# Block-sparse attention followed by a Swish MLP on one core: dummy matmuls at the head, one AV bank for both heads, earlier casts, and output steps that lag into the next group

## The chip, the cores and the metric

The kernel runs on one core of a Trainium2 chip. The metric is the device time of one execution in microseconds (us). Each kernel is executed several times; every execution that is compared here is fast, unless it is said otherwise (slow is an execution over 1.5% above the fastest of the same kernel). "The profile" is one traced execution; the span that it reports is about 2 us shorter than the measured time.

Engines: PE does matmuls (and 128-column transposes by a matmul with an identity), ACT does activations, DVE is the vector engine, POOL the general engine, and SP only issues transfers (DMA).

## The reference

```python
# q, k, v: (4 batches, 8 heads, 768 rows, 64); float32
scores = q @ k.T / 8, masked by 32x32 blocks          # band, first/last, 3 sampled
attn   = softmax(scores);   x = (attn @ v)            # -> x: (3072 tokens, 512)
h = x @ w_in                                          # 512 -> 2048
out = (h * sigmoid(beta * h)) @ w_out                 # 2048 -> 512
```

## The kernel before

A "pair" is two heads of one batch; there are 16 pairs. The rows of the four batches are cut into eight tiles of 512 or 256 rows, and for each tile the four pairs of its batch are worked one after the other. While a tile's attention runs, the MLP ("MoE" in the code) of the 512 tokens that were finished before is woven in: 16 up-projection steps (`h_step`) and 16 output steps (`o_step`), four matmuls of 512 columns each.

```python
tiles = [(0, 0, 512), (0, 512, 256), (1, 0, 256), (1, 256, 512),
         (2, 0, 512), (2, 512, 256), (3, 0, 256), (3, 256, 512)]
sc_pool: 2 buffers of 2 PSUM banks;  av_pool: 1 bank;  mm_pool: 3 banks

def emit_cast(x):                       # float32 loads -> float16
    ... cast K, Q; for pairs x >= 5: two DMA transposes on the SP queue ...
    nc.vector.tensor_copy(out=va[:, :, :, 0:D], in_=vst...)       # V as well

def av_step(hh):                        # one head: AV, then its normalisation
    av = av_pool.tile([P, 4, D + 1], FP32, tag="av", name="av")
    for qc in range(nq):
        for kc in range(NC): nc.tensor.matmul(av[:, qc, :], ...)
    nc.vector.reciprocal(...); nc.vector.tensor_tensor(... op=ALU.mult)
return steps, [av_step(0), av_step(1), turn]       # turn: transpose x on PE

# for pair x of a tile: when is the next pair cast?  One pair ahead:
if b == 0 or (b == 1 and q0 == 0): nxt = x + 1 ...
elif q0 + n == S and b + 1 < B:    nxt = x + NPAIR
slots[0 ...].append(lambda: (emit_cast(nxt), load_upto(nxt + 3)))

# one group's MLP: all h_steps, then all o_steps, spread over the score steps
backlog = moe_steps(gi * 512, 512)
```

Each score step is two or three matmuls into one of two score buffers (`sc`), and one exponential on ACT (`et<-sc`).

The softmax here doesn't subtract the row's maximum and nothing guards it: scores larger than these inputs give would overflow.

Of the kernel before, what the change touches and what calls it, by code (L numbers as in the profile page):

```python
# [17 lines left out]
def kernel(  # L18
# [14 lines left out]
    BLK = 32  # L33
# [23 lines left out]
    AUG = P - D  # L57
# [62 lines left out]
    oh_tok = persist.tile([P, NC, AUG], FP16, name="oh_tok")  # L120
    mask16 = persist.tile([NB, AUG], FP16, name="mask16")

    def emit_first():
# [7 lines left out]
        for j in range(3):  # L131
            emit_load(0, j)


# [9 lines left out]
        nc.gpsimd.memset(mask16, 0.0)  # L144

        nc.gpsimd.memset(onehot, 1.0)
        nc.gpsimd.affine_select(out=onehot, in_=onehot, pattern=[[1, NC], [NC, P]],
                                compare_op=ALU.is_ge, fill=0.0, base=0,
                                channel_multiplier=-BLK)
        nc.gpsimd.affine_select(out=onehot, in_=onehot, pattern=[[-1, NC], [-NC, P]],  # L150
                                compare_op=ALU.is_ge, fill=0.0, base=BLK - 1,
                                channel_multiplier=BLK)

        nc.gpsimd.memset(oh_tok, 1.0)
        nc.gpsimd.affine_select(out=oh_tok, in_=oh_tok, pattern=[[1, NC], [-BLK, AUG]],
                                compare_op=ALU.is_ge, fill=0.0, base=0,
                                channel_multiplier=NC)
        nc.gpsimd.affine_select(out=oh_tok, in_=oh_tok, pattern=[[-1, NC], [BLK, AUG]],
# [5 lines left out]
        nc.gpsimd.tensor_copy(out=ident32, in_=identity[0:16, 0:16])  # L164

# [16 lines left out]
        nc.vector.tensor_scalar(out=mask16[:, 0:NB], in0=mask_blk, scalar1=1.0,  # L182
                                scalar2=-NEG, op0=ALU.subtract, op1=ALU.mult)
        for i in range(NSTG):
            for h in range(2):
                nc.scalar.copy(out=stg["k"][i][:, h, :, D:P], in_=oh_tok)
            if i == 0:
                ps = mm_pool.tile([P, NC, AUG], FP32, tag="mm", name="mkt")
                for c in range(NC):
                    nc.tensor.matmul(ps[:, c, :], lhsT=oh_flat[:, c * P:(c + 1) * P],  # L190
                                     rhs=mask16, start=True, stop=True)
            for h in range(2):
                nc.scalar.copy(out=stg["q"][i][:, h, :, D:P], in_=ps)
# [13 lines left out]
    def emit_cast(x):  # L207
        b, j = seq[x]
        kst, qst, vst = loaded.pop((b, j))
        kX, qX = sets[x % NSET]  # L210
        va = va_tiles[x % NVA]
        for name, st32, dst in (("k", kst, kX), ("q", qst, qX)):
            st16 = stg[name][x % NSTG]
            nc.vector.tensor_copy(out=st16[:, :, :, 0:D],
                                  in_=st32.rearrange("p h (c d) -> p h c d", d=D))
            if x >= N_PE_PREP:
                nc.sync.dma_start_transpose(
                    out=dst.rearrange("p h (c s) -> p (h c) s", s=P),
                    in_=st16.rearrange("p h c e -> p (h c e)"))
        nc.vector.tensor_copy(out=va[:, :, :, 0:D],  # L220
                              in_=vst.rearrange("p h (c d) -> p h c d", d=D))
        prepared[(b, j)] = (kX, qX, va)

    def emit_turn(x, name, h):
        kX, qX, _ = prepared[seq[x]]
        dst = kX if name == "k" else qX
        st16 = stg[name][x % NSTG]
        tp = mm_pool.tile([P, NC, P], FP16, tag="mm", name="tp")
        for c in range(NC):
            nc.tensor.transpose(out=tp[0:D + NB, c, :], in_=st16[:, h, c, 0:D + NB],  # L230
                                identity=identity)
        nc.vector.tensor_copy(out=dst[0:D + NB, h, :],  # L232
                              in_=tp[0:D + NB].rearrange("p c s -> p (c s)"))

    def attn_steps(b, j, q0, n):
# [5 lines left out]
        def step(hh, kc0):  # L241
            def run():
                kX, qX, _ = prepared[(b, j)]
# [18 lines left out]
        def av_step(hh):  # L262
            def run():
                _, _, va = prepared[(b, j)]
                if hh == 0:
                    xst["t"] = work_pool.tile([P, 4, P], FP16, tag="xst", name="xst")
                xstage = xst["t"]
                av = av_pool.tile([P, 4, D + 1], FP32, tag="av", name="av")
                for qc in range(nq):
                    for kc in range(NC):  # L270
                        et, i = ets[hh][kc]
                        nc.tensor.matmul(av[:, qc, :],  # L272
                                         lhsT=et[:, i * n + qc * P:i * n + (qc + 1) * P],
                                         rhs=va[:, hh, kc, 0:D + 1],
                                         start=(kc == 0), stop=(kc == NC - 1))
                recip = work_pool.tile([P, 4], FP32, tag="recip", name="recip")
                nc.vector.reciprocal(out=recip[:, 0:nq], in_=av[:, 0:nq, D])  # L277
                nc.vector.tensor_tensor(  # L278
                    out=xstage[:, 0:nq, hh * D:(hh + 1) * D],
                    in0=av[:, 0:nq, 0:D],  # L280
                    in1=recip[:, 0:nq].to_broadcast([P, nq, D]),
                    op=ALU.mult)
            return run

        def turn():
            xstage = xst["t"]
            xtp = mm_pool.tile([P, 4, P], FP16, tag="mm", name="xtp")
            for qc in range(nq):
                nc.tensor.transpose(out=xtp[:, qc, :], in_=xstage[:, qc, :],  # L289
                                    identity=identity)  # L290
            nc.vector.tensor_copy(  # L291
                out=xT_sb[:, j, b * S + q0:b * S + q0 + n],
                in_=xtp[:, 0:nq, :].rearrange("p c s -> p (c s)"))

        return steps, [av_step(0), av_step(1), turn]


    def moe_steps(t0, n):
# [21 lines left out]
        def o_step(ts, quarter):  # L320
            def run():
# [17 lines left out]
        return ([h_step(f) for f in range(N_FFC)]  # L339
                + [o_step(ts, qq) for ts in range(n // P) for qq in range(4)])  # L340
# [19 lines left out]


    a_list = []
    behind = []
    seen = {0}
    tok = 0
    for b, q0, n in tiles:
        for j in range(NPAIR):
# [4 lines left out]
            if b == 0 or (b == 1 and q0 == 0):  # L372
                if x + 1 < 2 * NPAIR and x + 1 not in seen and (
                        j < NPAIR - 1 or q0 + n == S):
                    nxt = x + 1
            elif q0 + n == S and b + 1 < B:
                nxt = x + NPAIR
            seen.add(nxt)
            slots = [[] for _ in steps]
            last = len(steps) - 1  # L380
            for i, f in enumerate(behind):
                slots[min(i + 1, last)].append(f)
            if nxt is not None:
                slots[0 if b == 0 or q0 == 0 else last].append(
                    lambda nxt=nxt: (emit_cast(nxt), load_upto(nxt + 3)))
# [14 lines left out]
        tok += n  # L400
    for f in behind:
        a_list.append((0.0, f))

    with tc.manual_schedule():
        emit_first()
        emit_cast(0)
        load_upto(3)
        for name in ("k", "q"):
            for h in range(2):
                emit_turn(0, name, h)  # L410
        emit_beta()
        marks = [i for i, (w, f) in enumerate(a_list) if f == "mark"]
        backlog, per, acc, gi = [], 0.0, 0.0, 0
        for i, (w, f) in enumerate(a_list):
            if f == "mark":
                while backlog:
                    backlog.pop(0)()
                backlog = moe_steps(gi * 512, 512)
# [4 lines left out]
                continue  # L423
            f()
            acc += per * w
            while acc >= 1.0 and backlog:
                backlog.pop(0)()
                acc -= 1.0
        while backlog:
            backlog.pop(0)()  # L430
        for m in moe_steps((n_group - 1) * 512, 512):
            m()
# [30 lines left out]
```

## Time and profile before

325.17 us (median of 3 runs, 325.03 to 325.48).

The page of the kernel before: busy time of each engine, and three rows of the timeline in 40 equal slices (tenths busy; PEclk is the granted clock).

```profile
PE 292.4 (91%) x2527; PEld 162.7 (50%) x2527; DVE 143.6 (44%) x336; ACT 221.4 (69%) x289; POOL 13.0 (4%) x32
...
PE   2898789868799999999999999989999999989995
...
ACT  4588879665374988675997567887667896456711
...
PEclk9999999997799999999999999999999999999999
```

PE is the busiest engine. Busy PE is not the same as PE at its rate, so I also counted work: in this trace a matmul at full clock starts 215 ns (512 columns), 108 ns (256), 56 ns (128) or 32 ns (65, the AV matmuls) after the one before it. A stage's *work* is the sum of these costs; its *stall* is its length minus its work. The stages below start with the first score matmul of a tile. Over the whole span this gives 276.6 us of work and 46.3 us of stall. (The prediction counted AV at 29 ns, which moves 3 us from work to stall; here it is 32 for all kernels.)

| stage (rows of the batch) | start | length | work | stall |
|---|---|---|---|---|
| head | 0 | 11.3 | 1.8 | 9.5 |
| T0: batch 0, 512 | 11.3 | 26.9 | 19.6 | 7.3 |
| T1: batch 0, 256 | 38.2 | 25.0 | 19.5 | 5.5 |
| T2: batch 1, 256 | 63.2 | 31.6 | 20.7 | 10.9 |
| T3 and T4: 512 each | 94.9 | 95.4 | 93.2 | 2.2 |
| T5 and T6: 256 each | 190.2 | 46.2 | 41.5 | 4.6 |
| T7: batch 3, 512 | 236.4 | 54.9 | 52.6 | 2.4 |
| tail (last MLP group) | 291.3 | 27.7 | 27.6 | 0.1 |
| end (last eviction, transfer) | 319.0 | 3.8 | 0 | 3.8 |

The list of waits of PE, before (total us, times, longest):

```profile
PE av L272 <- DVE xst L278: 8.4, 16, 1.1
...
PE sc L246 <- ACT et L252: 3.0, 8, 0.5
PE sc L246 <- DMA qX_98<-qstg_77: 2.5, 1, 2.5
PE sc L246 <- DMA qX_96<-qstg_78: 2.1, 1, 2.1
PE xtp L289 <- DVE xst L278: 1.7, 4, 0.7
```

AV of the second head waits for the normalisation of the first (`xst`), since there is one AV bank. Twice PE waits for a DMA transpose (`qX<-qstg`). In the timeline of PE (start, duration, what, and in brackets the idle time before it and what ended that) these look so:

```profile
68.53 0.55 PE L272 MATMUL av<-va_73,et 128*128 128x65 f16 x12 [1.14 <-DVE xst L278]
...
72.45 0.49 PE L246 MATMUL sc<-qX_96,kX_95 88*128 88x256 f16 x3 [2.06 <-DMA qX_96<-qstg_78]
...
82.33 0.49 PE L246 MATMUL sc<-qX_98,kX_97 88*128 88x256 f16 x3 [2.54 <-DMA qX_98<-qstg_77]
```

After each of the two transfers' waits the trace has 3.4 us at half clock (the two 7s in the PEclk row). The first exponential, in the timeline of ACT:

```profile
12.35 1.94 ACT L252 ACTIVATE et<-sc 128x1024 f16<-128x1024 f32 x2 [3.11 <-PE sc L246]
```

### The profile page before, as it was taken

What the parts mean: (1) busy time and instruction counts of PE and PEld (TensorE: products, weight loads), DVE (VectorE), ACT (ScalarE), POOL (GpSimd) and SP (SyncE); (2) the same over time, 40 slices, a digit from 0 to 9 for tenths busy, and PEclk for the clock granted to TensorE, in tenths of its full rate; (3) what the DMA queues carried; (4) which work ended last, traced back from release to release, by engine and by line L of the source; (5) the groups of instructions that cost most, each with busy time, mean ns of one, the idle gap of its engine ahead of it and who ended that gap; (6) DMA issues with size and microseconds to landing.
All of it is one profiled execution on the core that took longest, in us unless ns stands there. A gap on an engine that the chain in (4) does not pass through costs nothing.

```text
span 322.8 us, 6109 instructions
## 1 busy us (share of the span) xinstructions
PE 292.4 (91%) x2527; PEld 162.7 (50%) x2527; DVE 143.6 (44%) x336; ACT 221.4 (69%) x289; POOL 13.0 (4%) x32
## 2 busy tenths in 40 slices
PE   2898789868799999999999999989999999989995
PEld 2555455534455455545545556545654545554442
DVE  6676245765121657332654115785122653116800
ACT  4588879665374988675997567887667896456711
POOL 6080000000000000000000000000000000000000
PEclk9999999997799999999999999999999999999999
DMA  6969993467961478788000116964101000110011
GB/s 179 376 125 207 197 361 109 146 120 201 266 200 46 83 196 207 173 242 244 3 0 2 47 53 100 275 121 77 36 34 67 0 2 1 66 65 2 0 67 65
DMA packets 55376, 38.41 MB, mean 119 GB/s; under 512 B 35877, under 2 KB 52277, under 8 KB 55349
## 3 DMA queue, kind: packets, MB, share of 16 engines
q1 hardware_dynamic: 51092, 33.82, 38.0%
q0 software_dynamic: 4224, 4.19, 8.0%
q8 instruction: 20, 0.33, 0.4%
q14 instruction: 8, 0.06, 0.0%
q10 hardware_dynamic: 32, 0.01, 0.0%
HBM read 27.27 MB, written 6.29 MB: 104 GB/s over the span
## 4 chain that ended last, share of the span: by engine, by line
PE 72%; ACT 11%; DVE 9%; DMA 4%; issue 3%; SPq 1%; ACTq 0%
PE op L327 25%; PE hp L308 18%; PE sc L246 15%; PE av L272 11%; ACT et L252 7%; ACT t_sb L313 3%; DVE g L315 3%; DVE xst L278 2%; PE xtp L289 2%; DMA vst<-in_v_dram 2%; PE tp L230 1%; DMA qX_98<-qstg_77 1%; DMA qX_96<-qstg_78 1%; DVE recip L277 1%; ACT osb L332 1%
## 5 line engine op out<-in xcount | busy, mean ns | idle before, releaser
L252 ACT ACTIVATE et<-sc 128x1024 f16<-128x1024 f32 (+1 forms) x160 | 148.3, 942 | 67.5 <-PE sc L246 66.5
L308 PE MATMUL hp<-xT_sb,w_in_sb 128*128 128x512 f16 x384 | 94.9, 381 | 0.0
L327 PE MATMUL op<-w_out_sb,g 128*128 128x512 f16 x384 | 94.3, 383 | 0.0
L315 DVE SCALAR_TENSOR_TENSOR g<-t_sb,hp 128x512 f16<-128x512 f16 x96 | 65.1, 687 | 55.5 <-ACT t_sb L313 54.7
L313 ACT ACTIVATE t_sb<-hp,beta_h_sb 128x512 f16<-128x512 f32 x96 | 65.8, 698 | 9.0 <-PE hp L308 7.6
L327 PEld LDWEIGHTS <-g 128*128 128x128 f16 x384 | 37.4, 98 | 41.6 <-issue 0.9
L272 PEld LDWEIGHTS <-et 128*128 128x128 f16 x1152 | 43.6, 98 | 27.4 <-DVE xst L278 17.2
L308 PEld LDWEIGHTS <-w_in_sb 128*128 128x128 f16 x384 | 37.3, 97 | 39.4 <-issue 0.8
L277 DVE RECIPROCAL recip<-av 128x4 f32<-128x4 f32 (+1 forms) x64 | 11.1, 174 | 84.5 <-PE av L272 84.5
L246 PE MATMUL sc<-qX_96,kX_95 88*128 88x512 f16 (+1 forms) x96 | 23.9, 349 | 3.0 <-DMA qX_96<-qstg_78 2.1
L332 ACT ACTIVATE osb<-op 128x512 f32<-128x512 f32 x24 | 14.3, 596 | 17.3 <-PE op L327 17.1
L278 DVE TENSOR_TENSOR xst<-av,recip 128x256 f16<-128x256 f32 (+1 forms) x64 | 22.9, 358 | 2.2
L246 PE MATMUL sc<-qX_98,kX_97 88*128 88x512 f16 (+1 forms) x72 | 16.7, 331 | 3.2 <-DMA qX_98<-qstg_77 2.5
L291 DVE COPY xT_sb<-xtp 128x512 f16<-128x512 f16 (+1 forms) x32 | 11.4, 356 | 15.0 <-PE xtp L289 15.0
L246 PE MATMUL sc<-qX_100,kX_99 88*128 88x512 f16 (+1 forms) x72 | 16.6, 325 | 0.7 <-ACT et L252 0.7
L246 PE MATMUL sc<-qX_102,kX_101 88*128 88x512 f16 (+1 forms) x72 | 16.3, 325 | 0.8 <-ACT et L252 0.7
L246 PE MATMUL sc<-qX_104,kX_103 88*128 88x256 f16 (+1 forms) x72 | 16.5, 326 | 0.2 <-DVE qX_104 L232 0.2
L272 PE MATMUL av<-va_70,et 128*128 128x65 f16 x288 | 11.8, 194 | 2.6 <-DVE xst L278 2.6
L289 PEld LDWEIGHTS <-xst 128*128 128x128 f16 x96 | 7.3, 98 | 10.9 <-DVE xst L278 5.7
L246 PEld LDWEIGHTS <-kX_95 88*128 88x128 f16 x96 | 8.5, 103 | 7.9 <-issue 4.7
L289 PE MATMUL xtp<-identity,xst 128*128 128x128 f16 x96 | 10.7, 220 | 1.7 <-DVE xst L278 1.7
L272 PE MATMUL av<-va_74,et 128*128 128x65 f16 x216 | 9.1, 196 | 1.9 <-DVE xst L278 1.9
(77 smaller groups left out, 134.6 us busy)
## 6 DMA issues: line engine op xcount, KB each, us to landing
kst<-in_k_dram SPq DMA_DIRECT2D x16, 384.0 KB, 3.9
qst<-in_q_dram SPq DMA_DIRECT2D x16, 384.0 KB, 4.8
vst<-in_v_dram SPq DMA_DIRECT2D x16, 384.0 KB, 5.5
out_dram<-osb SPq DMA_DIRECT2D x24, 256.0 KB, 2.0
w_in_sb<-in_moe_w_in_dram POOLq DMA_DIRECT2D x4, 512.0 KB, 8.4
w_out_sb<-in_moe_w_out_dram POOLq DMA_DIRECT2D x4, 512.0 KB, 16.6
kX_95<-kstg_76 SPq DMA_TRANSPOSE x2, 3.8
qX_96<-qstg_78 SPq DMA_TRANSPOSE x2, 4.0
```

The source lines that it names most:

```text
L246: nc.tensor.matmul(sc[:, i * n:(i + 1) * n], lhsT=kX[0:D + NB, hh, (kc0 + i) * P:(kc0 + i + 1) * P], rhs=qX[0:D + NB, hh, q0:q0 + n], star ...
L252: nc.scalar.activation(out=et[:, 0:kn * n], in_=sc[:, 0:kn * n], func=AF.Exp, bias=0.0, scale=SCALE)
L272: nc.tensor.matmul(av[:, qc, :], lhsT=et[:, i * n + qc * P:i * n + (qc + 1) * P], rhs=va[:, hh, kc, 0:D + 1], start=(kc == 0), stop=(kc == ...
L277: nc.vector.reciprocal(out=recip[:, 0:nq], in_=av[:, 0:nq, D])
L278: nc.vector.tensor_tensor(out=xstage[:, 0:nq, hh * D:(hh + 1) * D], in0=av[:, 0:nq, 0:D], in1=recip[:, 0:nq].to_broadcast([P, nq, D]), op= ...
L289: nc.tensor.transpose(out=xtp[:, qc, :], in_=xstage[:, qc, :], identity=identity)
L291: nc.vector.tensor_copy(out=xT_sb[:, j, b * S + q0:b * S + q0 + n], in_=xtp[:, 0:nq, :].rearrange("p c s -> p (c s)"))
L308: nc.tensor.matmul(hp[:, 0:n], lhsT=w_in_sb[:, c, f * P:(f + 1) * P], rhs=xT_sb[:, c, t0:t0 + n], start=(c == 0), stop=(c == NPAIR - 1))
L313: nc.scalar.activation(out=t_sb[:, 0:n], in_=hp[:, 0:n], func=AF.Tanh, bias=0.0, scale=beta_h_sb[:, f:f + 1])
L315: nc.vector.scalar_tensor_tensor(out=g[:, f, 0:n], in0=t_sb[:, 0:n], scalar=1.0, in1=hp[:, 0:n], op0=ALU.add, op1=ALU.mult)
L327: nc.tensor.matmul(op, lhsT=g[:, f, ts * P:(ts + 1) * P], rhs=w_out_sb[:, f, :], start=(f == 0), stop=(f == N_FFC - 1))
L332: nc.scalar.activation(out=osb, in_=op, func=AF.Copy, bias=0.0, scale=0.5)
```

## The change

Its intent: bring PE's clock up before the first real work; take work out of the head; end the AV waits by letting both heads of a tile share one AV bank and one normalisation; cast earlier, so that DMA transposes are ready; and mix PE-heavy output steps between the ACT-heavy up-projections. The core of the diff, with cuts:

```diff
+    def emit_warm(n): ... n matmuls of 512 columns on zeros, into a score buffer
 def emit_first():
-        nc.gpsimd: onehot by two affine_selects;  oh_tok 64 columns wide
+        oh_tok 24 columns wide; onehot = PE transpose of oh_tok, copied by ACT
+        emit_warm(6); ... transposes, copy ...; emit_warm(6)     # before the mask product
 def emit_cast(x):
-        V cast here
+    def emit_cast_v(x): ... V cast, now with the next load at the pair's last step
 def emit_turn(x, name, h, on_act=False):      # first Q copies run on ACT
@@ AV
-        def av_step(hh):          # one head, up to 4 row chunks
+        def av_step(half):        # two row chunks, both heads
-                av = av_pool.tile([P, 4, D + 1], FP32, tag="av", name="av")
+                av = av_pool.tile([P, 2, 2, D + 1], FP32, tag="av", name="av")
...
-        return steps, [av_step(0), av_step(1), turn]
+        return steps, [av_step(half) for half in range(nq // 2)] + [turn]
@@ MLP steps
+    N_LATE = 8
+    def mix(hs, late): ... two late o_steps first, the others spread between the h_steps
-                backlog = moe_steps(gi * 512, 512)
+                hs, os = moe_steps(gi * 512, 512)
+                backlog = mix(hs, late) + os[:N_LATE]
+                late = os[N_LATE:]                      # 8 of 16 go to the next group
@@ which pair is cast
-            if b == 0 or (b == 1 and q0 == 0): nxt = x + 1 ...
+            if b == 0 and q0 == 0:
+                if j < NPAIR - 1: nxt = x + 1
+            elif b == 0 and j >= 2 or b == 1 and q0 == 0 and j < 2: nxt = x + 2
...
-                slots[min(i + 1, last)].append(f)
+                slots[1 + 2 * i if len(behind) == 2 or last == 5 else i + 1].append(f)
...
-                    lambda nxt=nxt: (emit_cast(nxt), load_upto(nxt + 3)))
+                    lambda nxt=nxt: emit_cast(nxt))
+                slots[last].append(lambda nxt=nxt: (emit_cast_v(nxt), load_upto(nxt + 3)))
@@ end
+    n_hold = 5      # output steps kept for between the last AV steps ("two")
-        for m in moe_steps((n_group - 1) * 512, 512): m()
+        for m in mix(hs, late) + os: m()
```

More of the change, by code (lines that the diff above doesn't have):

```diff
@@ L56 @@
     NSTG = 2
-    AUG = P - D
     va_tiles = []
@@ L119, with emit_warm @@
     oh_flat = onehot.rearrange("j c p -> j (c p)")
-    oh_tok = persist.tile([P, NC, AUG], FP16, name="oh_tok")
-    mask16 = persist.tile([NB, AUG], FP16, name="mask16")
+    oh_tok = persist.tile([P, NC, NB], FP16, name="oh_tok")
+    mask16 = persist.tile([NB, NB], FP16, name="mask16")
+    warm = persist.tile([P, 512], FP16, name="warm")
+    sc_warm = []
+    def emit_warm(n):
+        if not sc_warm:
+            sc_warm.append(sc_pool.tile([P, 1024], FP32, tag="sc", name="warm_ps"))
+        for _ in range(n):
+            nc.tensor.matmul(sc_warm[0][:, 0:512], lhsT=warm[:, 0:P], rhs=warm,
+                             start=True, stop=True)
     def emit_first():
@@ L132, in emit_first @@
             emit_load(0, j)
+        nc.vector.memset(warm, 0.0)
         dif = persist.tile([NB, NB], FP32, name="dif")
@@ L143, in emit_first @@
                        allow_small_or_imprecise_dtypes=True)
-        nc.gpsimd.memset(mask16, 0.0)
-        nc.gpsimd.memset(onehot, 1.0)
-        nc.gpsimd.affine_select(out=onehot, in_=onehot, pattern=[[1, NC], [NC, P]],
-                                compare_op=ALU.is_ge, fill=0.0, base=0,
-                                channel_multiplier=-BLK)
-        nc.gpsimd.affine_select(out=onehot, in_=onehot, pattern=[[-1, NC], [-NC, P]],
-                                compare_op=ALU.is_ge, fill=0.0, base=BLK - 1,
-                                channel_multiplier=BLK)
         nc.gpsimd.memset(oh_tok, 1.0)
-        nc.gpsimd.affine_select(out=oh_tok, in_=oh_tok, pattern=[[1, NC], [-BLK, AUG]],
+        nc.gpsimd.affine_select(out=oh_tok, in_=oh_tok, pattern=[[1, NC], [-BLK, NB]],
                                 compare_op=ALU.is_ge, fill=0.0, base=0,
                                 channel_multiplier=NC)
-        nc.gpsimd.affine_select(out=oh_tok, in_=oh_tok, pattern=[[-1, NC], [BLK, AUG]],
+        nc.gpsimd.affine_select(out=oh_tok, in_=oh_tok, pattern=[[-1, NC], [BLK, NB]],
                                 compare_op=ALU.is_ge, fill=0.0, base=BLK - 1,
@@ L164, in emit_first @@
         nc.gpsimd.tensor_copy(out=ident32, in_=identity[0:16, 0:16])
+        for i in range(NSTG):
+            for nm in ("k", "q"):
+                nc.gpsimd.memset(stg[nm][i][:, :, :, D + NB:P], 0.0)
+        emit_warm(6)
+        ohp = mm_pool.tile([P, NC, P], FP16, tag="mm", name="ohp")
+        for c in range(NC):
+            nc.tensor.transpose(out=ohp[0:NB, c, :], in_=oh_tok[:, c, :], identity=identity)
+        nc.scalar.copy(out=oh_flat, in_=ohp[0:NB].rearrange("j c p -> j (c p)"))
+        emit_warm(6)
         mask_blk = persist.tile([NB, NB], FP32, name="mask_blk")
@@ L181, in emit_first, with emit_more_columns @@
                                            op0=ALU.is_equal, op1=ALU.max)
-        nc.vector.tensor_scalar(out=mask16[:, 0:NB], in0=mask_blk, scalar1=1.0,
+        nc.vector.tensor_scalar(out=mask16, in0=mask_blk, scalar1=1.0,
                                 scalar2=-NEG, op0=ALU.subtract, op1=ALU.mult)
-        for i in range(NSTG):
-            for h in range(2):
-                nc.scalar.copy(out=stg["k"][i][:, h, :, D:P], in_=oh_tok)
-            if i == 0:
-                ps = mm_pool.tile([P, NC, AUG], FP32, tag="mm", name="mkt")
-                for c in range(NC):
-                    nc.tensor.matmul(ps[:, c, :], lhsT=oh_flat[:, c * P:(c + 1) * P],
-                                     rhs=mask16, start=True, stop=True)
-            for h in range(2):
-                nc.scalar.copy(out=stg["q"][i][:, h, :, D:P], in_=ps)
+        for h in range(2):
+            nc.scalar.copy(out=stg["k"][0][:, h, :, D:D + NB], in_=oh_tok)
+        ps = mm_pool.tile([P, NC, NB], FP32, tag="mm", name="mkt")
+        for c in range(NC):
+            nc.tensor.matmul(ps[:, c, :], lhsT=oh_flat[:, c * P:(c + 1) * P],
+                             rhs=mask16, start=True, stop=True)
+        for h in range(2):
+            nc.scalar.copy(out=stg["q"][0][:, h, :, D:D + NB], in_=ps)
+    def emit_more_columns():
+        for i in range(1, NSTG):
+            for nm in ("k", "q"):
+                for h in range(2):
+                    nc.scalar.copy(out=stg[nm][i][:, h, :, D:D + NB],
+                                   in_=stg[nm][0][:, h, :, D:D + NB])
     def emit_beta():
@@ L219, in emit_cast, with emit_cast_v, emit_turn @@
                     in_=st16.rearrange("p h c e -> p (h c e)"))
+        prepared[(b, j)] = (kX, qX, va, vst)
+    def emit_cast_v(x):
+        _, _, va, vst = prepared[seq[x]]
         nc.vector.tensor_copy(out=va[:, :, :, 0:D],
                               in_=vst.rearrange("p h (c d) -> p h c d", d=D))
-        prepared[(b, j)] = (kX, qX, va)
-    def emit_turn(x, name, h):
-        kX, qX, _ = prepared[seq[x]]
+    def emit_turn(x, name, h, on_act=False):
+        kX, qX, _, _ = prepared[seq[x]]
         dst = kX if name == "k" else qX
@@ L231, in emit_turn @@
                                 identity=identity)
-        nc.vector.tensor_copy(out=dst[0:D + NB, h, :],
-                              in_=tp[0:D + NB].rearrange("p c s -> p (c s)"))
+        copy = nc.scalar.copy if on_act else nc.vector.tensor_copy
+        copy(out=dst[0:D + NB, h, :], in_=tp[0:D + NB].rearrange("p c s -> p (c s)"))
     def attn_steps(b, j, q0, n):
@@ L242, in run @@
             def run():
-                kX, qX, _ = prepared[(b, j)]
+                kX, qX, _, _ = prepared[(b, j)]
                 sc = sc_pool.tile([P, 1024], FP32, tag="sc", name="sc")
@@ L260, in attn_steps @@
         xst = {}
-        def av_step(hh):
+        def av_step(half):
             def run():
-                _, _, va = prepared[(b, j)]
-                if hh == 0:
-                    xst["t"] = work_pool.tile([P, 4, P], FP16, tag="xst", name="xst")
-                xstage = xst["t"]
-                av = av_pool.tile([P, 4, D + 1], FP32, tag="av", name="av")
-                for qc in range(nq):
-                    for kc in range(NC):
-                        et, i = ets[hh][kc]
-                        nc.tensor.matmul(av[:, qc, :],
-                                         lhsT=et[:, i * n + qc * P:i * n + (qc + 1) * P],
-                                         rhs=va[:, hh, kc, 0:D + 1],
-                                         start=(kc == 0), stop=(kc == NC - 1))
-                recip = work_pool.tile([P, 4], FP32, tag="recip", name="recip")
-                nc.vector.reciprocal(out=recip[:, 0:nq], in_=av[:, 0:nq, D])
+                _, _, va, _ = prepared[(b, j)]
+                if half == 0:
+                    xst["t"] = work_pool.tile([P, 4, 2, D], FP16, tag="xst", name="xst")
+                av = av_pool.tile([P, 2, 2, D + 1], FP32, tag="av", name="av")
+                for i in range(2):
+                    qc = half * 2 + i
+                    for hh in range(2):
+                        for kc in range(NC):
+                            et, m = ets[hh][kc]
+                            nc.tensor.matmul(av[:, i, hh, :],
+                                             lhsT=et[:, m * n + qc * P:m * n + (qc + 1) * P],
+                                             rhs=va[:, hh, kc, 0:D + 1],
+                                             start=(kc == 0), stop=(kc == NC - 1))
+                recip = work_pool.tile([P, 2, 2, 1], FP32, tag="recip", name="recip")
+                nc.vector.reciprocal(out=recip, in_=av[:, :, :, D:D + 1])
                 nc.vector.tensor_tensor(
-                    out=xstage[:, 0:nq, hh * D:(hh + 1) * D],
-                    in0=av[:, 0:nq, 0:D],
-                    in1=recip[:, 0:nq].to_broadcast([P, nq, D]),
+                    out=xst["t"][:, half * 2:half * 2 + 2],
+                    in0=av[:, :, :, 0:D],
+                    in1=recip.to_broadcast([P, 2, 2, D]),
                     op=ALU.mult)
@@ L288, in turn @@
             for qc in range(nq):
-                nc.tensor.transpose(out=xtp[:, qc, :], in_=xstage[:, qc, :],
+                nc.tensor.transpose(out=xtp[:, qc, :], in_=xstage[:, qc].rearrange("p h d -> p (h d)"),
                                     identity=identity)
@@ L337, in o_step @@
             return run
-        return ([h_step(f) for f in range(N_FFC)]
-                + [o_step(ts, qq) for ts in range(n // P) for qq in range(4)])
+        return ([h_step(f) for f in range(N_FFC)],
+                [o_step(ts, qq) for ts in range(n // P) for qq in range(4)])
     tiles = [(0, 0, 512), (0, 512, 256), (1, 0, 256), (1, 256, 512),
@@ L359, in load_upto, with mix @@
             n_loaded[0] += 1
+    N_LATE = 8
+    def mix(hs, late):
+        res, rest = late[:2], late[2:]
+        done = 0
+        for i, h in enumerate(hs):
+            res.append(h)
+            while done < len(rest) and done * len(hs) < (i + 1) * len(rest):
+                res.append(rest[done])
+                done += 1
+        return res
     a_list = []
     behind = []
-    seen = {0}
     tok = 0
@@ L371 @@
             nxt = None
-            if b == 0 or (b == 1 and q0 == 0):
-                if x + 1 < 2 * NPAIR and x + 1 not in seen and (
-                        j < NPAIR - 1 or q0 + n == S):
+            if b == 0 and q0 == 0:
+                if j < NPAIR - 1:
                     nxt = x + 1
-            elif q0 + n == S and b + 1 < B:
+            elif b == 0 and j >= 2 or b == 1 and q0 == 0 and j < 2:
+                nxt = x + 2
+            elif b > 0 and q0 + n == S and b + 1 < B:
                 nxt = x + NPAIR
-            seen.add(nxt)
             slots = [[] for _ in steps]
@@ L400 @@
         tok += n
+    n_hold = 5
     for f in behind:
         a_list.append((0.0, f))
+        a_list.append((0.0, "two"))
     with tc.manual_schedule():
@@ L406 @@
         emit_cast(0)
-        load_upto(3)
         for name in ("k", "q"):
             for h in range(2):
-                emit_turn(0, name, h)
+                emit_turn(0, name, h, on_act=(name == "q"))
+        emit_more_columns()
+        emit_cast_v(0)
+        load_upto(3)
         emit_beta()
         marks = [i for i, (w, f) in enumerate(a_list) if f == "mark"]
-        backlog, per, acc, gi = [], 0.0, 0.0, 0
+        backlog, late, per, acc, gi = [], [], 0.0, 0.0, 0
         for i, (w, f) in enumerate(a_list):
@@ L423 @@
                 continue
+            if f == "two":
+                for m in backlog[:2]:
+                    m()
+                backlog = backlog[2:]
+                continue
             f()
             acc += per * w
-            while acc >= 1.0 and backlog:
+            while acc >= 1.0 and len(backlog) > (n_hold if gi == len(marks) else 0):
                 backlog.pop(0)()
                 acc -= 1.0
-        while backlog:
-            backlog.pop(0)()
-        for m in moe_steps((n_group - 1) * 512, 512):
+        for m in backlog:
+            m()
+        hs, os = moe_steps((n_group - 1) * 512, 512)
+        for m in mix(hs, late) + os:
             m()
```

## The prediction

> **What bounds it now.** The tensor engine (PE). The start-to-start costs of all matmuls at full clock, read from the trace (512 columns 215 ns, 256: 108, 128: 56, 65: 29), sum to 273 of the 322.8 us span. The rest is 6.3 us before the first matmul, about 40 us of stalls between matmuls and 3.7 us after the last. The change can only win stalls. They lie here (timeline of PE, list of waits):
> - 0 to 20 us: 6.1 us on top of the 6.3. V's cast (its load lands at 8.5 us) stands on DVE ahead of the first K copies; the first exponential starts at 12.35 us.
> - 20 to 44 us: 6.7 us. Attention without MoE work: ACT runs 24 exponentials, 0.94 us apart, with idles of 0.4 to 0.65 us.
> - 44 to 95 us: 15.1 us. AV waits for the previous head's normalisation (single AV bank, up to 1.3 us each, about 4 us); two waits for DMA transposes cast only one pair ahead (2.2 and 2.7 us); after each one 3.4 us stretch at half clock, about 3.4 us together.
> - 95 to 195 us: 3.4 us. 195 to 222: 3.9, of them 3.3 AV behind its normalisation. 222 to 288: 2.4. After 288: 2.1, the last AV/normalise/transpose chain.
>
> **What the change does.**
> - Casts for DMA-transposed pairs come two pairs ahead: the transpose takes 4 us, the pair before it over 6. Both DMA waits and half-clock stretches go: 8 us, the largest gain. The Trainium skill ("TensorE: Matmul & The Clock Gate", Part 1) says an idle window of about 3.4 us drops the clock to half; the clock row here agrees (0.7 in two slices, after waits of 2 to 3 us).
> - 256-row tiles do AV once for both heads: no AV behind normalisation there. About 4 us in the first such stage, 3 in the second, minus what ACT then binds.
> - Late output steps thin the first stage: 8 of its 16 output steps (0.86 us each, 6.9 us) move on to later groups and finally to the dense tail. That is a transfer, no gain; mixing them between up-projections helps only where ACT binds.
> - Head: no V cast and less POOL work in front, Q copies on ACT; against it 12 dummy matmuls (0.43 us each cold) before the mask product in PE order, and four column copies on ACT before the first exponential. I expect that at 11 us: gain 1 to 2 us, and 1.5 to 2 more from AV and transposes spread over steps 1, 3, 5.
> - End: output steps held between the last AV steps: gain 1.3.
> - New: a half-finished output accumulation holds one of three "mm" banks while up-projections take 2.5 us each from first matmul to freed bank; where a bank returns after two of them (twice in the tail) about 0.8 us is lost. I charge 2 us there, 1 to 2 elsewhere.
>
> Sum: 3.5 + 11 + 2.4 + 1.3 + 1 - 2 = 17 to 19. Predicted 307 us, range 300 to 313. Chances: faster 0.95, same 0.04, slower 0.01.
>
> **Signs.** Right: no DMA transpose among PE's releasers and no half-clock slice after the head; AV's wait for normalisation below 2 us in total; first exponential at 10 to 11.5 us; PE's matmul work unchanged but for the dummies; the first 512-row score of the second batch near 75 us instead of 95. Wrong: ACT without idle but PE waiting from 40 to 75 us (ACT-bound), or up-projections waiting for DVE's g over 4 us in total (bank shortage).
>
> **What would break it.** Late loads for the earlier casts (pair 4's lands at 44 to 46 us); bank shortage in every stage; dummies delaying the mask product beyond 7.5 us.

## The result, and the profile after

314.42 us (median of 4 runs, 313.93 to 314.81), beside 325.14 us for the kernel before: 10.7 us less. The ratio is 0.9668 (95% interval 0.9651 to 0.9684). Ratios are the mean time of one kernel's fast runs over that of the other's of the same rounds, so not quite the ratio of the medians quoted. The direction was right; the time lies above the predicted range of 300 to 313.

The page after:

```profile
PE 291.8 (94%) x2545; PEld 163.7 (52%) x2545; DVE 139.0 (45%) x303; ACT 221.7 (71%) x292; POOL 10.7 (3%) x32
...
PE   8799889987999999999989999999999899899995
...
ACT  3998877984678879668776689889587786255511
...
PEclk9999999997999999999999999999999999999999
```

The waits of PE, after:

```profile
PE sc L265 <- DMA qX<-qstg: 3.6, 2, 2.2
PE hp L328 <- DVE g L335: 3.0, 4, 0.9
PE sc L265 <- ACT et L271: 2.1, 7, 0.4
PE tp L249 <- DVE kstg L230: 1.9, 2, 1.0
...
PE xtp L309 <- DVE g L335: 1.1, 4, 0.3
...
PE av L292 <- DVE xst L298: 0.4, 1, 0.4
```

AV's wait for its normalisation has gone from 8.4 to 0.4 us. The waits for DMA transposes have not gone: two, of 3.6 us in total. And a new line stands second: up-projections (`hp`) wait for DVE's `g`, that is, for a bank of the "mm" pool. Lines from PE's timeline that show both, and one near the end:

```profile
66.58 0.60 PE L265 MATMUL sc<-qX,kX 88*128 88x256 f16 x4 [1.40 <-DMA qX<-qstg]
...
72.98 0.49 PE L265 MATMUL sc<-qX,kX 88*128 88x256 f16 x3 [2.17 <-DMA qX<-qstg]
...
266.29 0.62 PE L292 MATMUL av<-va,et 128*128 128x65 f16 x14 [0.68 <-ACT et L271]
...
284.06 1.02 PE L328 MATMUL hp<-xT_sb,w_in_sb 128*128 128x512 f16 x4 [0.64 <-DVE g L335]
...
290.90 1.02 PE L328 MATMUL hp<-xT_sb,w_in_sb 128*128 128x512 f16 x4 [0.64 <-DVE g L335]
```

The first exponential, in ACT's timeline:

```profile
10.09 4.66 ACT L271 ACTIVATE et<-sc 128x1024 f16<-128x1024 f32 x5
```

Where the time came from, by stage. The work of the head grew by 2.9 us (the dummies and the six transposes of the mask helper), so there the length counts. The tail is counted from the last transpose of the attention (271.1 us after); in the changed kernel one held output step of the group before still falls in it.

| stage | length before | after | stall before | stall after |
|---|---|---|---|---|
| head | 11.3 | 8.7 | 9.5 | 4.0 |
| T0 | 26.9 | 24.8 | 7.3 | 5.2 |
| T1 | 25.0 | 21.4 | 5.5 | 4.5 |
| T2 | 31.6 | 24.5 | 10.9 | 6.3 |
| T3 and T4 | 95.4 | 93.2 | 2.2 | 2.5 |
| T5 and T6 | 46.2 | 44.2 | 4.6 | 1.8 |
| T7 | 54.9 | 54.4 | 2.4 | 2.7 |
| tail | 27.7 | 37.0 | 0.1 | 1.7 |

T1 and T2 are also shorter because 5.1 us of output steps left them; the tail's length grew by that kind of work (nine steps, 7.7 us) and by 1.6 us of stall. Stalls fell by 13.8 us in all and work rose by 2.9. What I had counted on and did not get is in two places: T1 and T2 (predicted 11 us, got 5.6), and the late stages with the tail (predicted a small gain, got 2.2 us of loss: T3, T4, T7 and tail went from 4.7 to 6.9).

### The profile page after: what moved, and what is told of

It reads as the page before. It is cut to its first block, busy times and chain, and to the rows that moved or that the text cites. A ratio compares the mean times of both kernels' runs of the same rounds, so it can differ in the third digit from the quotient of the medians.

```text
span 311.9 us, 6116 instructions
## 1 busy us (share of the span) xinstructions
PE 291.8 (94%) x2545; PEld 163.7 (52%) x2545; DVE 139.0 (45%) x303; ACT 221.7 (71%) x292; POOL 10.7 (3%) x32
## 4 chain that ended last, share of the span: by engine, by line
PE 78%; ACT 11%; DVE 5%; DMA 3%; issue 2%; ACTq 0%
PE op L347 27%; PE hp L328 21%; PE sc L265 15%; PE av L292 10%; ACT et L271 6%; ACT t_sb L333 4%; DVE g L335 3%; DMA qX<-qstg 3%; PE tp L249 2%; PE warm_ps L128 1%; PE xtp L309 1%; DVE xst L298 1%; ACT qX L252 0%; DVE kstg L230 0%; PE ohp L173 0%
## 5 line engine op out<-in xcount | busy, mean ns | idle before, releaser
L347 PE MATMUL op<-w_out_sb,g 128*128 128x512 f16 x384 | 94.9, 381 | 0.4 <-DVE g L335 0.4
L265 PE MATMUL sc<-qX,kX 88*128 88x512 f16 (+1 forms) x384 | 87.4, 326 | 6.2 <-DMA qX<-qstg 3.6
L265 PEld LDWEIGHTS <-kX 88*128 88x128 f16 x384 | 33.3, 98 | 25.7 <-issue 9.6
L292 PE MATMUL av<-va,et 128*128 128x65 f16 x1152 | 44.8, 193 | 1.2 <-ACT et L271 0.7
L297 DVE RECIPROCAL recip<-av 128x4 f32<-128x4 f32 x48 | 8.6, 180 | 35.1 <-PE av L292 35.0
L298 DVE TENSOR_TENSOR xst<-av,recip 128x256 f16<-128x256 f32 x48 | 20.4, 424 | 1.7
L311 DVE COPY xT_sb<-xtp 128x512 f16<-128x512 f16 (+1 forms) x32 | 11.3, 354 | 16.1 <-PE xtp L309 15.9
L230 DVE CAST qstg<-qst 128x768 f16<-128x768 f32 x16 | 9.1, 571 | 0.5 <-DMA qst<-in_q_dram 0.5
L230 DVE CAST kstg<-kst 128x768 f16<-128x768 f32 x16 | 9.0, 562 | 0.7 <-DMA kst<-in_k_dram 0.7
L240 DVE CAST va<-vst 128x768 f16<-128x768 f32 x16 | 8.8, 552 | 0.3 <-DMA vst<-in_v_dram 0.3
L249 PE MATMUL tp<-identity,kstg 128*88 128x128 f16 x60 | 4.9, 220 | 1.9 <-DVE kstg L230 1.9
L249 PEld LDWEIGHTS <-kstg 128*88 128x88 f16 x60 | 4.1, 120 | 3.4 <-ACT qstg L208 1.4
```

The costliest lines, as they stand in the source:

```text
L230: nc.vector.tensor_copy(out=st16[:, :, :, 0:D], in_=st32.rearrange("p h (c d) -> p h c d", d=D))
L249: nc.tensor.transpose(out=tp[0:D + NB, c, :], in_=st16[:, h, c, 0:D + NB], identity=identity)
L265: nc.tensor.matmul(sc[:, i * n:(i + 1) * n], lhsT=kX[0:D + NB, hh, (kc0 + i) * P:(kc0 + i + 1) * P], rhs=qX[0:D + NB, hh, q0:q0 + n], star ...
L292: nc.tensor.matmul(av[:, i, hh, :], lhsT=et[:, m * n + qc * P:m * n + (qc + 1) * P], rhs=va[:, hh, kc, 0:D + 1], start=(kc == 0), stop=(kc ...
L298: nc.vector.tensor_tensor(out=xst["t"][:, half * 2:half * 2 + 2], in0=av[:, :, :, 0:D], in1=recip.to_broadcast([P, 2, 2, D]), op=ALU.mult)
L347: nc.tensor.matmul(op, lhsT=g[:, f, ts * P:(ts + 1) * P], rhs=w_out_sb[:, f, :], start=(f == 0), stop=(f == N_FFC - 1))
```

## The experiments

Theory 1: the transposes stay late because the DMA engines are full in T2, by the loads of later pairs; casting earlier attacks a delay where a rate is the limit. Theory 2: the lag is no neutral transfer; it thins T1 and T2, and its half-finished output tile takes one of three banks. Rivals: (B) the casts or the transposes are late of themselves; (for the lag) it helps where ACT binds. All experiments are edits of the changed kernel (314.42). Every run below gave a correct result. Runs of the kernel before beside them had medians of 324.95 to 325.62 us.

### e1: the loads of pairs 8 and 9 behind the transposes

```diff
-                slots[last].append(lambda nxt=nxt: (emit_cast_v(nxt), load_upto(nxt + 3)))
+                slots[last].append(lambda nxt=nxt: (emit_cast_v(nxt),
+                    None if nxt in (5, 6) else load_upto(nxt + 3)))
```

> The changed kernel, with the K, Q and V loads of pairs 8 and 9 (third batch, first needed 20 us later) issued only together with those of pair 10, behind the DMA transposes of pairs 5 to 7 in the one SP queue. Theory A (the queue is full: 3 loads and 2 transposes take about 7.2 us a pair there, a pair of 256-row tiles lasts 5 to 6 us, so transposes cast two pairs ahead still fall behind): both waits of PE for a DMA transpose (1.6 and 2.3 us) and the half-clock stretch (1.7 us) go, 308.5 to 310.5 us. Rival B (the casts on DVE come too late, or a transpose takes its 5 to 7 us whatever else is queued): both waits stay, 313.5 to 315.

Measured: 309.03 us (308.75 to 309.52), ratio 0.9499 (0.9471 to 0.9527): 5.4 us less. The SP queue after the change, in the window where PE waits (start, duration of the issue):

```profile
58.50 2.31 SPq L233 DMA_TRANSPOSE kX<-kstg  x1
60.90 2.69 SPq L233 DMA_TRANSPOSE qX<-qstg  x1
63.64 0.93 SPq L76 DMA_DIRECT2D kst<-in_k_dram  x1
...
65.70 2.77 SPq L233 DMA_TRANSPOSE kX<-kstg  x1
68.56 2.54 SPq L233 DMA_TRANSPOSE qX<-qstg  x1
```

The same in e1:

```profile
58.79 1.43 SPq L233 DMA_TRANSPOSE kX<-kstg  x1
60.31 1.94 SPq L233 DMA_TRANSPOSE qX<-qstg  x1
63.86 1.37 SPq L233 DMA_TRANSPOSE kX<-kstg  x1
65.32 1.79 SPq L233 DMA_TRANSPOSE qX<-qstg  x1
```

After the change a pair takes 7.2 us of the queue (58.50 to 65.70) while pairs follow each other every 5 to 6 us; without the loads, issues are shorter and each pair is done before the next comes. The waits for transposes shrink to 0.3 us, no half-clock stretch is left before the last matmul, and the stall of T2 goes from 6.3 to 1.2 us with every other tile's stage the same to 0.1. In the view of the tile `qX` between 40 and 80 us, e1 has:

```profile
  DMA qX<-qstg: 0.3, 1
...
DMA to landing us min/median/max: 4.1/4.3/5.3
```

The loads are the cause: without them in between, the waits go, though the casts come at the same steps, so that late casts (rival B) are not it. But the last line says where the time went. From its issue a Q transpose lands no sooner than in the changed kernel (4.1/4.3/5.5, shown under e3). What shrank is the time before: the Q of pair 7 (counted from 0, the last pair of T2) is issued 4.6 us after its cast has ended in the changed kernel (68.56 against 63.97), 1.1 us in e1 (65.32 against 64.26). Whether the queue's order or the DMA engines behind it set that pace, e1 does not say.

### e2: casts one pair ahead again

```diff
-            elif b == 0 and j >= 2 or b == 1 and q0 == 0 and j < 2:
-                nxt = x + 2
+            elif b == 0 and j == 3 or b == 1 and q0 == 0 and j < 3:
+                nxt = x + 1
```

> The changed kernel with casts for pairs 4 to 7 one pair ahead again, as in the kernel before. If the earlier cast is worth what the stage table says (pair 5's wait of 2.2 us gone, others shifted), the time goes up by 2 to 5 us, to 316.5 to 319.5, with two waits for transposes and two half-clock stretches. If the earlier cast was worth nothing because the queue limits either way: 314 to 315.

Measured: 320.08 us (319.34 to 320.13), ratio 0.9832. The earlier cast is worth 5.7 us within this change. The list of waits of e2:

```profile
PE sc L265 <- DMA qX<-qstg: 8.3, 3, 4.0
```

The rise is a little above the expected 2 to 5 us, and there are three waits, not two. Their sum is more than the 4.6 us of the kernel before, with the same look-ahead. The likely reason, not tested by itself, is that T2 has less PE work under which to hide a transpose (18.2 us here, 20.7 before). Two half-clock stretches are there too, as before.

### e3: the same loads, issued from another queue

```diff
-            emit_load(*seq[y])
+            emit_load(*seq[y], eng=nc.gpsimd if y in (8, 9, 10) else None)
```

> The changed kernel with the nine loads of pairs 8 to 10 issued from the POOL queue at the same places of the program, so that they no longer stand in front of transposes in the SP queue but still move the same bytes at the same time. If the order in the SP queue and its issue time is what delays the transposes: the waits shrink below 1 us in total, 309 to 311. If the shared DMA engines are what is full: the transposes still land 5 us and more after issue, waits stay near 4 us, 313 to 315.

Measured: 315.03 and 318.96 us in two fast runs, 331.05 and 327.95 in two slow ones, so its time is inconclusive and only the trace is used. In the view of the tile `qX` between 40 and 80 us, the time from issue to landing of a Q transpose (min/median/max) is, after the change:

```profile
DMA to landing us min/median/max: 4.1/4.3/5.5
```

and in e3:

```profile
DMA to landing us min/median/max: 7.0/7.9/9.3
```

No load stands in front of a transpose in the SP queue now, and yet the transposes land later, and PE waits 3.5 us for them, nearly the 3.6 of the changed kernel (at pairs 5 and 6 instead of 6 and 7). This speaks against the queue's order and for the shared engines. The Trainium skill says the same ("DMA: Bandwidth & Descriptors", "Issuing engines are not separate DMA queues"): transfers started by any engine run on the same 16 DMA engines and interleave. An estimate from the packet records of the changed kernel fits: spread over 16 engines, the packets of one pair's two transposes took 4.4 us and those of one pair's loads 3.6 us, together 8 us (somewhat too much, since packets overlap), where PE works a pair in 5 to 6. In 5 us windows from 55 to 70 us it moved 252, 211 and 321 GB/s, e1 132, 159 and 195. The mean DMA engine's busy share tells less: 1.07 to 1.16 in the changed kernel (transfers overlap), but 0.75, 1.19 and 1.05 in e1, so transposes alone reach such shares. A caution: POOL's loads were cut in another way (the nine took 1008 packets, against 2448 on the SP queue), so e3 does not move quite the same traffic. Shared engines are the better supported reading, not a proven one.

### e4: no dummy matmuls

```diff
-        emit_warm(6)
         ohp = mm_pool.tile([P, NC, P], FP16, tag="mm", name="ohp")
...
-        emit_warm(6)
```

> The changed kernel without its twelve dummy matmuls. If they pay by bringing the clock up early: the 24 head transposes run at half clock (56 ns more each, 1.3 us), the first exponential comes at 10.8 to 11.5 instead of 10.1, and the time goes up by 0.7 to 1.5 us. If the gain of the head came from the V cast moved away and the shorter POOL work alone: no change, or 0.3 us faster since the mask product no longer queues behind dummies.

Measured: 314.6 us (313.12 to 315.61), ratio 0.9665 (0.9626 to 0.9705): no difference that three rounds show. The head lasted 9.5 us, not 8.7, and the first exponential came at 10.9; but this trace happened to have no half-clock stretch in T2, though PE waited 3.6 us for transposes there too. See e10.

### e5: no lag

```diff
-    N_LATE = 8
+    N_LATE = 16
```

> The changed kernel with no lag: all 16 output steps stay in their own group. The late steps only transfer 6.9 us of PE work to the tail, so if they gain nothing where PE is the limit and cost bank waits (0.8 us twice in the tail, about 1 us each in the 512-row stages), this is 0 to 2 us faster, 312.5 to 314.5. If mixing output steps between up-projections is what keeps PE busy where ACT binds (first stages), this is 2 to 4 us slower, 316.5 to 318.5, with more stall in the 256-row stages.

Measured: 304.05 us (303.5 to 304.38), ratio 0.9336 (0.9295 to 0.9376): 10.4 us faster than the change with the lag. Neither expectation allowed for so much. The lag was the largest loss in the whole change. The waits of e5:

```profile
PE sc L265 <- ACT et L271: 3.0, 8, 0.8
PE sc L265 <- DMA qX<-qstg: 1.9, 2, 1.0
...
PE hp L328 <- DVE g L335: 0.6, 3, 0.2
```

With the output steps of the first group back in T1 and T2 (5.1 us of work; the last two run in T3), the transposes have more work to hide under (3.6 to 1.9 us, no half clock before the last matmul), and the waits for a bank fall from 3.0 to 0.6. By stage, stall with the lag and without: T1 4.5 and 3.3, T2 6.3 and 2.5, T3 and T4 2.5 and 1.1, T5 and T6 1.8 and 0.5, T7 2.7 and 1.8, tail 1.7 and 0.1. The work is the same 279.5 us.

### e6: AV one head at a time again

```diff
-                av = av_pool.tile([P, 2, 2, D + 1], FP32, tag="av", name="av")
+                av = av_pool.tile([P, 4, D + 1], FP32, tag="av", name="av")
...
-        return steps, [av_step(half) for half in range(nq // 2)] + [turn]
+        return steps, [av_step(0), av_step(1), turn]
```

> The changed kernel with AV one head at a time again, as before the change, with everything else kept. If the shared bank is worth the AV waits of the 256-row stages (before: about 4 us in the first such stage, 3 in the second): 4 to 7 us slower, 318.5 to 321.5, with AV behind its normalisation as PE's largest wait. If ACT or the transposes would bind there anyway: under 2 us slower.

Measured: 321.74 us (320.49 to 322.75), ratio 0.9872: 7.3 us slower. The list of waits of e6:

```profile
PE av L290 <- DVE xst L296: 9.7, 11, 1.8
```

The shared bank is worth 7 us, as I had costed it in total, but not in its parts (4 in the first 256-row stages, 3 in the later ones): against the changed kernel, stall rises by 3.2 us in T1 and T2 and by 5.5 in T5 and T6. In T2 the waits for AV take the place of those for transposes, of which e6 has none. With two heads a pair also has three late steps instead of two, which then stand closer together, as they did in the kernel before.

### e7: late output steps first, in the tail

```diff
-        for m in mix(hs, late) + os:
+        for m in late + hs + os:
```

> The changed kernel with the last group's eight late output steps run before its up-projections, not mixed among them. In the tail no exponential runs, and the mix makes a bank come back after two up-projections twice (0.8 us each in the trace). If that is bank shortage: 1.4 to 1.7 us faster. If the stall is ACT or DVE being late at those places: no change.

Measured: 312.46 us (312.01 to 314.9), ratio 0.9613: about 2 us faster, though its interval (0.9545 to 0.9681) overlaps that of the changed kernel. The trace is the surer sign: the tail's stall goes from 1.7 to 0.1; that this run also waited 0.9 us less for transposes has nothing to do with the edit. An up-projection takes about 2.5 us from its first matmul to its freed bank, and 0.86 us of PE; three banks in turn just suffice (three times 0.86 is 2.6), and where the output tile holds one of them, PE waits. The kernel's PSUM has no ninth bank to give: the score buffers use four, AV one and "mm" three, and the Trainium skill ("PSUM — Partial Sum Buffer", "Specifications (TRN2)") has 8 banks in all; the built program's tiles lie in banks 0 to 7.

### e8: pace without the held steps

```diff
-                per = len(backlog) / max(
+                per = (len(backlog) - (n_hold if gi == len(marks) else 0)) / max(
```

> The changed kernel with the pace of the last stage reckoned without the five output steps that are held back for its end. Now the pace uses the backlog up early, and an AV step near 265 us waits 1.1 us for exponentials with no output step between. If so: 0.7 to 1.3 us faster. If ACT is simply the limit of those last steps: no change.

Measured: 312.7 us (311.24 to 312.93), ratio 0.9595: 1.7 us faster, a little more than expected. T7's stall goes from 2.7 to 1.0. The held steps were meant to fill the gaps between the last AV steps; but the pace still counted them, so the others ran out before the last three score steps, and AV then waited for exponentials (the line at 266.29 us above).

### e11: the lag kept, but never half-way through an output tile

```diff
-                backlog = mix(hs, late) + os[:N_LATE]
+                backlog = late + hs + os[:N_LATE]
...
-        for m in mix(hs, late) + os:
+        for m in late + hs + os:
```

> The changed kernel with its lag of eight output steps kept, but run before the group's up-projections instead of mixed among them, in every group and in the tail. This parts the two costs of the lag. If the half-finished output tile that holds a bank is the cost: the up-projections' waits for DVE's g (3.0 us in four) go, the stalls of the 512-row and later 256-row stages and of the tail fall to those of the no-lag run, 310 to 312 us, while the first two 256-row stages and their waits for transposes stay as they are. If the cost is only the thinned first stages: no change, 313.5 to 315.

Measured: 310.61 us (310.39 to 310.8), ratio 0.9529 (0.9486 to 0.9572): 3.8 us faster. The waits of e11:

```profile
PE sc L265 <- DMA qX<-qstg: 3.7, 2, 2.2
...
PE hp L328 <- DVE g L335: 0.8, 4, 0.2
```

The bank waits go, the waits for transposes stay, and T1 and T2 stall as in the changed kernel (4.5 and 6.4). All of PE's waits for `g`, that is, for a "mm" bank, sum to 5.1 us in the changed kernel (`hp`, `xtp`, `op` and `tp`) and 1.4 here, which is the same 3.7. So 3.8 of the lag's 10.4 us are the held bank.

### e9 and e10: the repaired kernel, with and without dummies

e9 takes the changed kernel with the edits of e1, e5 and e8. e10 is e9 without the two `emit_warm(6)`. They ran on one chip, five rounds each.

> The changed kernel with three repairs: no lag, loads of pairs 8 and 9 issued behind the transposes of pairs 5 to 7, and the last stage paced without the five held steps. If the causes are separate and the stage table adds up, the no-lag run (304.05) loses its remaining 1.9 us of waits for transposes and 0.9 us of the last stage: 301 to 302 us. If pacing or the queue trade waits for others: 303 to 305.

> The same with the twelve dummy matmuls taken out. In the profiled runs so far the head lasts 8.6 to 9.6 us with dummies, following the moment at which the clock came up (4.1 to 7.2 us), and 9.5 without them (clock up at 11.0). So the dummies should be worth 0 to 0.9 us, about 0.3 on average: 0 to 0.6 us slower than the run beside it. If they are worth what the change intended, over 1 us slower.

Measured: e9 301.22 us (300.34 to 301.95), ratio 0.9245 (0.9214 to 0.9276); e10 302.19 us (301.1 to 302.44), ratio 0.9268 (0.9238 to 0.9298). e9 beats both kernels: 13.2 us under the change and 24 us under the kernel before. Its page:

```profile
PE 288.7 (96%) x2545; PEld 164.1 (55%) x2545; DVE 138.3 (46%) x303; ACT 219.4 (73%) x292; POOL 10.6 (4%) x32
...
PE   8799899999999999999999999999999999999995
...
PEclk9799999999999999999999999999999999999998
```

Its two largest waits of PE (no transfer is left in the list; waits for a bank, `hp` and `tp`, are 0.6 us each):

```profile
PE sc L265 <- ACT et L271: 2.2, 7, 0.4
PE tp L249 <- DVE kstg L230: 1.6, 1, 1.6
```

From T2 on, all stages together stall 2.6 us. What is left is the head, T0 (where ACT has 24 exponentials and there is no MLP work yet) and T1. In this one profiled run the clock fell to half once more at 11.7 us, after PE had waited for a cast; this run took 301.95. Of the timed runs beside it, all five without dummies (302.0 to 302.44) are above all five with them (300.34 to 301.94), by 1.1 us in the mean. The two profiled runs go the other way (301.95 with, 301.1 without), and the intervals of the two ratios overlap, so I put the dummies' worth at 1 us at most (0.75 with the profiled runs counted in).

### e12: the lag put back into the repaired kernel

The edits of e1, e8 and e11 together, so the lag has neither the held bank nor the loads between the transposes against it.

> The repaired kernel (301.22) with the lag of eight output steps put back, in the form that does not hold a bank (late steps before the up-projections) and with the loads deferred, so that neither bank shortage nor the waits for transposes can be blamed. If the lag is then only a transfer of PE work to the tail: 301 to 302 us. If thinning the first 256-row stages still costs there, because ACT and the chains bind sooner (stall of those two stages 4.5 and 1.2 us with the lag, 3.3 and 0.3 without): 302.5 to 304. If lag pays once its side costs are gone: under 300.5.

Measured: 303.46 us (302.94 to 305.92), ratio 0.9367 (0.9314 to 0.9419): 2.2 us slower than e9, but on another chip. Set against the kernel before, the difference is larger (ratio 0.9367 against 0.9245, about 4 us), and from T1 on the two traces differ by about 3 us of stall; so the sign is sure, the size is 2 to 4 us. T1 and T2 stall 4.5 and 1.2 us, with e9's at 3.3 and 0.3. There the 5.1 us of output steps that left T1 and T2 made those two stages only 3.0 us shorter (40.8 against 43.8 us), while the same work costs its full time in the tail. The lag never paid in any form that was run.

## Why the prediction was wrong

- **What bounds it: right.** PE's work is unchanged but for the dummies and mask transposes (276.6 to 279.5 us), and the change won only stalls.
- **Head and T0, predicted 3.5 us: 4.7, part of it luck.** The head of this trace, 8.7 us, is at the short end of what the eleven traces with dummies show (8.6 to 9.6, median 9.3), so 4.1 is nearer the mark; of that the dummies are worth no more than about 1 us (e4, e10). The first exponential came at 10.09 us (forecast 10 to 11.5; 12.35 before).
- **AV at normalisation: right in sum.** The wait fell to 0.4 us, and e6 puts the part at 7.3 us, more of it in the later stages than forecast.
- **"Both DMA waits and half-clock stretches go: 8 us" failed.** By the prediction's own count they were 2.2, 2.7 and 3.4 us; after, 1.6 and 2.3 us of wait (start to start less the cost of one matmul, so 0.2 us more each than the idle times shown) and 1.7 us of half clock remained, so the step gave 2.7 of 8.3 us. I compared the delay of one transpose (4 us) with the length of one pair (over 6 us). That is right for a single transfer. But a pair has two, one behind the other (5.6 us from the first issue, at 66.69, to the second landing in the kernel before), and T2 brings three pairs after one another, with the loads of three more between them. Together they took longer than PE needs for a pair: 7.2 us of the queue, for want of room on the DMA engines as far as e3 shows, and pairs had become shorter. e1 gets the rest back: 5.4 us.
- **"That is a transfer, no gain" failed, and cost most.** The lag loses 10.4 us (e5): 3.8 by the held bank (e11), 2.2 (2 to 4, see e12) by thinning stages where PE was not alone the limit and paying the work again in the tail (e12 against e9), and by subtraction 4.4 (less, if thinning costs more) by exposing the transposes, of which T2's stall in e5 (3.8 us less) is the direct sign. The last overlaps with the 5.4 us of e1: either repair alone covers most of those waits. The two failed steps are thus one fault of reasoning: I costed the parts of the change singly, and one part took away the PE work under which another was to hide.
- **Bank shortage: right mechanism, size short.** I charged 2 us in the tail and 1 to 2 elsewhere, but put only 2 into the sum; 3.8 us were measured. The "wrong" sign that I named, up-projections waiting for `g` over 4 us, did not come in as worded: they waited 3.0 us. Only with the transposes and output steps, which take banks of the same pool, is it 5.1.
- **"End: gain 1.3" failed.** T7's stall rose from 2.4 to 2.7, since the pace counted the held steps; e8 shows 1.7 us to be had. With the pace mended T7 stalls 1.0, a gain of 1.4: the idea was right, the count was not.
- **Sign at T3: half right.** Its first score came at 79.4 us, not near 75 (94.9 before). In e1 it came at 74.6.

With the DMA step as forecast (e1), the time would have been 309, inside the range. The range was missed by 1.4 us only, so each repair alone (e1, e5, e7, e8, e11) brought the time into it; what counts is the size of the two failed steps.

## What to carry to other kernels

Work that is moved out of a stage is filler taken from every transfer that the stage hides: before you call a move neutral, ask what ran underneath it, and what limits the stage that it leaves and the stage that it goes to. When a transfer arrives late, see which others share its queue and its engines; beside starting it earlier (worth 5.7 us here, e2), put off the loads that nobody needs yet (5.4 us, e1). An accumulation left half-done holds its bank, so count the banks that are left against the time for which each is in use.

## What the Trainium skill lacked or had wrong

- "TensorE: Matmul & The Clock Gate", Part 1, gives about 3.4 us of idleness for the drop to half clock. Here shorter ones did: the start-to-start gap of PE's matmuls before a drop was 2.0 to 2.6 us in seven traces (2.4 after the change, 2.0 in e9 at 9.2 us), 2.3 and 2.8 in the kernel before, 3.2 and 4.2 in e2. One gap of 2.2 us and one of 1.8 caused none (e4). Each drop lasted 3.4 us, as the page has it.
- The same page says that the window is free-running, so that the moment of warming varies, and gives the spread as 500 ns to either side. The traces agree that it varies, but by 3.1 us, and put a price on it: with the same twelve dummies the full clock came between 4.1 and 7.2 us, and the head lasted 8.6 to 9.6 us accordingly.
- "DMA: Bandwidth & Descriptors" has a bandwidth for DMA transposes, but not how long they take beside other transfers. Here one of 384 KB (128 x 12 x 128 values of 2 bytes) between two places of SBUF landed 3.8 to 4.1 us after its issue in the kernel before, where its pair's loads came behind it (pairs 5 and 6), and 7.0 to 9.3 us with loads beside it (Q in e3). Loads are not all of it: in e1 the two of pair 6 took 5.5 and 5.3 us with no load near them, for a reason that no run shows.
